# A product of the last matmul goes back from two levels of splitting to one, and the attention steps of the fourth unit are laid in another order

## The chip, the cores and the metric

One core of one Trainium2 chip runs the whole kernel. Times are device microseconds of that core. TensorE multiplies into PSUM[...], VectorE and ScalarE take the sums out of PSUM and do the elementwise work, and SyncE issues nearly all DMA transfers from one queue.

## The reference, cut to what matters

An attention without softmax is followed by a block of two matrix products with a squared relu between them. All arrays are fp32.

```python
kv  = einsum('bhsd,bhse->bhde', k, v)             # batch 8, heads 8, seq 576, head_dim 64
out = einsum('bhsd,bhde->bhse', q, kv)
out = out / sqrt(mean(out * out, -1) + 1e-6) * g_norm
x   = out.transpose(0, 2, 1, 3).reshape(4608, 512)
h   = x @ w_in                                    # 512 -> 2048
g   = s * maximum(h, 0) ** 2 + b
y   = g @ w_out                                   # 2048 -> 512
```

## The kernel before

The 4608 rows are cut into 36 chunks of 128, four chunks to a unit, so there are 9 units, numbered 0 to 8. The fourth unit is unit 3. In a unit the kernel does two big products, and inside the first it prepares the four attention chunks of the next unit.

Both products use a scheme of Winograd's: the matrices are cut into 2 x 2 blocks, sums of blocks are formed on VectorE, and seven block products take the place of eight. The first product (`mm1`) runs over four slices `s` of 512 columns. Its block products are named x1, z2, x6, y7, x5, x3 and y4 after the PSUM tiles x, y and z that they add into; block 3 of a slice and block 4 follow in the next slice, and for the last slice they follow in `rest()` below.

The second product (`mm2`) has seven block products too, numbered 1 to 7. From unit 2 on, six of them (1, 2, 6, 7, 4 and 3) are split a second time in the same way, into seven small products of 128 columns; only block 5 is done whole, with 256 columns for each of the two halves `j` of the rows. The second level of one block is made by `second_level`. `sums` forms the sums of the left matrix on VectorE, and `m1` to `m4` do the small products:

```python
def sums(which=(5, 6, 7, 3)):                 # each one is a 128x512 operation of VectorE
    ...
def go(m, bank, first):                       # four matmuls of 128 columns
    ...
    for f in range(FC // 4):
        matmul(t[bank], a[m][:, f], w[:, f], first and f == 0, f == FC // 4 - 1)

def keep(name, j, q):                         # a copy out of bank x, scaled, plus another term
    r[name] = late["tmp"].tile([P, P], FP32, name="r", tag="r")
    scaled(r[name], t["x"], other(j, cols[q]))

def m1(): go(1, "x", True);  keep("r1", 0, 0)
def m2(): go(2, "z", True);  scaled(to(0, cols[0]), t["z"], r["r1"])
def m6(): go(6, "x", False); keep("r2", 1, 0)          # adds to what m1 left in x
def m7(): go(7, "y", True)
def m5(): go(5, "x", False); keep("r4", 1, 1); scaled(to(1, cols[1]), t["y"], r["r4"])
def m3(): go(3, "x", False); scaled(to(0, cols[1]), t["x"], other(0, cols[1]))
def m4(): go(4, "y", False); scaled(to(1, cols[0]), t["y"], r["r2"])
```

Products 1, 6, 5 and 3 add into one bank, and each partial sum is copied out before the next product adds to it. `scaled` is one SCALAR_TENSOR_TENSOR operation of VectorE (line 714).

The order of a unit's second product stands in `rest()`. `p1`, `p2`, `p6`, `p7`, `p3`, `p4` are the second levels of the blocks; `at(n)` puts in a step of the next unit's attention, `at(5)` the four sums of the next unit's x; `pump(n)` asks for the next n tiles of weights, in a ring of 7. Its last part, from unit 2 on:

```python
            p7[2](); pump(1)
            p7[6]()
            p3["sums"]((5, 6))
            p7[7](); pump(1)
            p7[5]()
            at(3)
            p3["sums"]((7, 3))
            at("sums")
            p7[3](); pump(1)
            p7[4](); pump(1)
            with_5(0)                         # o1 += o2, the part from block 5
            at(("q", 0))
            p3[1](); p4["sums"]((5, 6)); at("norm")
            p3[2](); with_5(1); pump(1)
            p3[6](); p4["sums"]((7, 3))
            p3[7](); pump(1)
            p3[5]()
            at(4)
            p4[1]()
            p3[3](); store("o1", 0, 4 * u); pump(1)
            p3[4](); store("o1", 1, 4 * u + 1); pump(1)
            at(5)                             # the four sums of the next unit's x
            p4[2]()
            p4[6]()
            with_7(0)
            p4[7]()
            with_7(1)
            p4[5](); pump(2)
            at(("q", 1))
            y4_of(0, 3); pump(1)              # p4[3] and a store of o2
            y4_of(1, 4); pump(1)              # p4[4] and a store of o2
            at(("q", 2))
```

The attention steps of the next unit stand in a table: the key is (slice, place in the slice), and the places are 0 before x1, 1 after z2, 2 after x6 and 3 after y7. `turn` transposes q of a chunk on VectorE, `product` multiplies with kv on TensorE and squares on ScalarE, `row_sum` and `norm` (a square root on ScalarE, a reciprocal and a product on VectorE) divide, and `turn_x` transposes the result back on VectorE; for every second chunk four scalings with g_norm on ScalarE follow. In the last slice of a unit p1's four sums are laid after y7, ahead of place 3.

Of the kernel before, what the change touches and what calls it, by code (L numbers as in the profile page):

```python
# [16 lines left out]
def kernel(  # L17
# [39 lines left out]
    nc = tc.nc  # L57
# [231 lines left out]


    w2_dram = [dram.tile([P, FC // 2, HN], FP32, name=f"w2_{i}") for i in range(8)]
    TWICE = (1, 2, 6, 7, 4, 3)
    w3_dram = {
        i: dram.tile([P, 7, FC // 4, P], FP32, name=f"w3_{i}") for i in TWICE
    }
# [100 lines left out]
    def attention(c, first=False):  # L396
# [32 lines left out]
        def product(with_sum=True):  # L429
            if first:  # L430
                ps = bank_of("att", "xy"[c % 2]).rearrange("p b (m n) -> p (b m) n", m=2)
            else:
                pool, tag = (ps_f, "y") if c == 17 or c > 19 and c % 2 else (ps_a, "x")
                ps = pool.tile([P, NP, P], FP32, name="x_ps", tag=tag)
            if c < 2:
                for p in range(NP):
                    matmul(ps[:, p, :], st["qT"][:, p, :], bd_kv[0][:, p, :], True, True)
            for w in range(4 if c >= 2 else 0):
                for p in range(NP):
                    nc.tensor.matmul(  # L440
                        ps[32 * p : 32 * p + 32, w, :],
                        lhsT=st["qT"][:, p, 32 * w : 32 * w + 32],
                        rhs=bd_kv[(b if w < 2 else b1) % 2][:, p, :],
                        start=True,
                        stop=True,
                    )
            st["x"] = ps.rearrange("p c (l d) -> p (c l) d", l=2)
            st["xn"] = attp.tile([P, H, D], FP32, name="xn", tag="xn")
            nc.scalar.activation(st["xn"], st["x"], AF.Square)
            if with_sum:  # L450
                row_sum()
# [94 lines left out]
    def relu_sq(t):  # L546
        nc.vector.scalar_tensor_tensor(t, t, 0.0, t, ALU.max, ALU.mult)  # L547
# [38 lines left out]
    def mm1(u, s):  # L586

        st = {}

        def keep(name, src, tag):  # L590
            st[name] = rp.tile([P, 2, TB], FP32, name=name, tag=tag)
            nc.scalar.copy(st[name], src)  # L592

        def x1():
            st["x"] = bank_of("x", "x")
            mm1_product(1, u, s, st["x"], True)
            keep("r1", st["x"], "ra")

        def z2():
            ps = bank_of("z", "z", 1)  # L600
            mm1_product(2, u, s, ps, True)
            t = g_tile("a11", s)
            add(t, ps, st["r1"])
            relu_sq(t)

        def x6():
            mm1_product(6, u, s, st["x"], False)
            keep("r2", st["x"], "rb")

        def y7():  # L610
            st["y"] = bank_of("y", "y")
            mm1_product(7, u, s, st["y"], True)

        def x5():
            mm1_product(5, u, s, st["x"], False)
            keep("r4", st["x"], "ra")
            t = g_tile("a22", s)
            add(t, st["y"], st["r4"])
            if u > 1 and s == NS - 1:
                nc.scalar.activation(t, t, AF.Relu)  # L620
                nc.scalar.square(t, t)
            else:
                relu_sq(t)

        def x3():
            mm1_product(3, u, s, st["x"], False)
            nc.scalar.activation(g_tile("a21", s), st["x"], AF.Relu)

        def x3_square():
            if u > 1 and s == NS - 1:  # L630
                nc.scalar.square(ga["a21", s], ga["a21", s])
            else:
                nc.vector.tensor_mul(ga["a21", s], ga["a21", s], ga["a21", s])

        def x3_s1():
            g_tile("s1", s)
            g_s1(s)

        def x3_s3():
            sub(ga["a21", s], ga["a11", s], ga["a21", s])  # L640

        def y4():
            mm1_product(4, u, s, st["y"], False)
            add(g_tile("a12", s), st["y"], st["r2"])

        def y4_square():
            relu_sq(ga["a12", s])

        return dict(
            x1=x1, z2=z2, x6=x6, y7=y7, x5=x5, x3=x3, x3_square=x3_square, x3_s1=x3_s1,  # L650
            x3_s3=x3_s3, y4=y4, y4_square=y4_square,
        )
# [41 lines left out]
    def mm2(u, step=None, side={}):  # L694
# [9 lines left out]
        def product(i, j, ps, first):  # L704
            for f in range(FC // 2):
                s, b = divmod(f, 2)
                w2 = W2_AT[i][:, f] if u == 0 else ring[u, i, f // 4][:, f % 4]
                matmul(
                    ps, ga[G_OF[i], s][:, b, j * P : j * P + P], w2,
                    first and f == 0, f == FC // 2 - 1,  # L710
                )

        def scaled(o, ps, other):
            nc.vector.scalar_tensor_tensor(o, ps, s_col, other, ALU.mult, ALU.add)  # L714
# [165 lines left out]
            if last(j):  # L880
                store("o2", j, 4 * u + 2 + j, slice(HN, DM))

        def x3(j):
            product(3, j, st["x", j], False)
            scaled(rows("o1", j)[:, HN:], st["x", j], b2 if u == 1 else st["o1", j][:, HN:])
            store("o1", j, 4 * u + j)

# [42 lines left out]
        if u == 1:  # L930
            return [
                seq(lambda: x1(0), lambda: parts_of_w(1)),
                seq(lambda: x1(1), lambda: pump(2), s2),
                seq(lambda: z2(0), lambda: parts_of_w(2)),
                seq(lambda: z2(1), lambda: pump(2), s4),
                seq(lambda: x6(0), lambda: parts_of_w(6)),
                seq(lambda: x6(1), lambda: pump(2)),
                seq(lambda: y7(0), lambda: parts_of_w(7)),
                seq(lambda: y7(1), lambda: pump(2)),
                lambda: x5(0),  # L940
                seq(lambda: x5(1), lambda: pump(2)),
                seq(lambda: x3(0), lambda: parts_of_w(3)),
                seq(lambda: x3(1), lambda: pump(2)),
                seq(lambda: y4(0), lambda: parts_of_w(4)),
                seq(lambda: y4(1), lambda: pump(2)),
            ]

        def right(name, j, q=slice(0, HN)):
            return rows(name, j)[:, HN:][:, q]
# [8 lines left out]
            4, lambda j, q: st["r2"][:, j, q], lambda j, q: rows("o2", j)[:, q], "t", "t"  # L958
        )

        p3 = second_level(3, lambda j, q: right("o1", j, q), lambda j, q: right("o1", j, q), "x")

        def x5_of(j, *between):
            st["x", j] = half(("x", j), "x")
            product(5, j, st["x", j], True)
            for fn in between:
                fn()
            scaled(right("o2", j), st["x", j], b_21)

        def with_5(j):  # L970

            add(right("o1", j), right("o1", j), right("o2", j))

        def with_7(j):

# [11 lines left out]
        def rest():  # L987
# [7 lines left out]
            pump(1)  # L995
            p1[5]()
            step["x3"]()
            step["x3_square"]()
            p2["sums"]()
            p1[3]()  # L1000
            pump(1)
            p1[4]()
            pump(1)
            at(0)
# [33 lines left out]
            s4((3,))  # L1038
            p6[4]()
            pump(1)  # L1040
            p7["sums"]((3,))
            p7[2]()
            pump(1)
            p7[6]()
            p3["sums"]((5, 6))
            p7[7]()
            pump(1)
            p7[5]()
            at(3)
            p3["sums"]((7, 3))  # L1050
            at("sums")
            p7[3]()
            pump(1)
            p7[4]()
            pump(1)
            with_5(0)
            at(("q", 0))
            p3[1]()
            p4["sums"]((5, 6))
            at("norm")  # L1060
            p3[2]()
            with_5(1)
            pump(1)
            p3[6]()
            p4["sums"]((7, 3))
            p3[7]()
            pump(1)
            p3[5]()
            at(4)
            p4[1]()  # L1070
            p3[3]()
            store("o1", 0, 4 * u)
            pump(1)
            p3[4]()
            store("o1", 1, 4 * u + 1)
            pump(1)
            at(5)
            p4[2]()
            p4[6]()
            with_7(0)  # L1080
            p4[7]()
            with_7(1)
            p4[5]()
            pump(2)
            at(("q", 1))
            y4_of(0, 3)
            pump(1)
# [186 lines left out]
    def sides(u):  # L1274
# [34 lines left out]
        else:  # L1309
# [8 lines left out]
            if u > 3:  # L1318
                first[1, 2] = [*turn[2:], *row_sum[:2]]
                first[2, 0] = [*turn_x[:2], *q[1]]  # L1320
                first.update({
                    (2, 1): product[2:],
                    (2, 2): row_sum[2:],
                    (2, 3): norm[2:],
                    (3, 0): [turn_x[2]],
                    (3, 1): [turn_x[3]],
                })
            else:
                first[2, 0] = [*turn_x[:2], turn[2]]
                first.update({  # L1330
                    (2, 1): [product[2], row_sum[2]],
                    (2, 2): [norm[2]],
                    (2, 3): [turn_x[2], turn[3], *q[1]],
                    (3, 0): [product[3], row_sum[3]],
                    (3, 1): [norm[3]],
                    (3, 2): [turn_x[3]],
                })
        second[5] = [lambda: [sums() for sums in x_sums(u + 1)]]
        return first, second
# [92 lines left out]
```

## Time and profile before

| what | before |
|---|---|
| time, median of 3 | 971.71 us (970.51 to 973.76) |
| span of the profiled execution | 968.4 us |
| granted TensorE clock | 0.999 |
| VectorE SCALAR_TENSOR_TENSOR, 128x128 out of PSUM | 0.35 us |
| VectorE SCALAR_TENSOR_TENSOR, 128x256 out of PSUM | 0.48 us |
| VectorE sum, 128x512 | 0.69 us |
| ScalarE copy out of PSUM, 128x512 | 0.58 us |
| a 512 KB tile of weights, issue to landing | 4.6 us (median) |

In the timeline a fp32 matmul leaves two records, so a group of four matmuls is written as x8. Names in the profile are those of the program with the numbers left out: `sub` are the sums that `sums` makes, `w_sb` is a tile of weights in the ring (`w2_sb` in the program), `r` a kept partial sum, `a` one of the tiles a11 to a22 of the first product's result. Line 91 is the helper through which nearly all matmuls go, line 440 the attention's product, line 714 `scaled`, line 818 the stores of the output.

### The profile page before, as it was taken

What the parts mean: (1) busy time and instruction counts of PE and PEld (TensorE: products, weight loads), DVE (VectorE), ACT (ScalarE), POOL (GpSimd) and SP (SyncE); (2) the same over time, 40 slices, a digit from 0 to 9 for tenths busy, and PEclk for the clock granted to TensorE, in tenths of its full rate; (3) what the DMA queues carried; (4) which work ended last, traced back from release to release, by engine and by line L of the source; (5) the groups of instructions that cost most, each with busy time, mean ns of one, the idle gap of its engine ahead of it and who ended that gap; (6) DMA issues with size and microseconds to landing.
All of it is one profiled execution on the core that took longest, in us unless ns stands there. A gap on an engine that the chain in (4) does not pass through costs nothing.

```text
span 968.4 us, 18270 instructions
## 1 busy us (share of the span) xinstructions
PE 938.0 (97%) x7438; PEld 842.9 (87%) x7438; DVE 659.6 (68%) x1220; ACT 204.8 (21%) x387; POOL 6.7 (1%) x18
## 2 busy tenths in 40 slices
PE   7999999999999999999999999999999999999997
PEld 6888888888889988888889988998889888988996
DVE  2789766586658855777477856785678667864585
ACT  3773132112231013300231013201330032001100
POOL 2000000000000000000000000000000000000000
PEclk9999999999999999999999999999999999999999
DMA  9688736588863775167544754377427800681075
GB/s 238 209 303 247 247 88 180 132 282 229 233 178 110 244 193 154 18 219 226 143 102 146 253 172 112 111 245 210 110 53 243 249 20 12 219 263 52 19 220 165
DMA packets 140835, 165.85 MB, mean 171 GB/s; under 512 B 78032, under 2 KB 93648, under 8 KB 140624
## 3 DMA queue, kind: packets, MB, share of 16 engines
q1 hardware_dynamic: 137648, 162.91, 56.8%
q10 hardware_dynamic: 2784, 1.77, 0.8%
q8 instruction: 59, 0.97, 0.4%
q14 instruction: 24, 0.20, 0.1%
q0 software_dynamic: 320, 0.00, 0.0%
HBM read 136.84 MB, written 27.79 MB: 170 GB/s over the span
## 4 chain that ended last, share of the span: by engine, by line
PE 81%; DVE 10%; DMA 4%; ACT 2%; issue 1%; SPq 1%; DVEq 0%; ACTq 0%
PE x_ps L91 36%; PE y_ps L91 25%; PE z_ps L91 8%; PE t_ps L91 7%; PE x_ps L440 3%; DMA w_sb<-w 2%; DVE xs L250 2%; PE kv_ps L377 1%; DVE r L714 1%; DMA w_raw<-in_moe_w_in_dram 1%; DVE sub L250 1%; ACT xT L494 1%; DMA kv_sb<-in_k_dram 1%; DVE xT L488 1%; DVE a L247 1%
## 5 line engine op out<-in xcount | busy, mean ns | idle before, releaser
L592 ACT COPY r<-x_ps 128x512 f32<-128x512 f32 x96 | 56.0, 583 | 419.2 <-PE x_ps L91 396.9
L91 PE MATMUL x_ps<-xs,ws 128*128 128x256 f32 x512 | 122.1, 381 | 0.8 <-ACT r L592 0.4
L91 PE MATMUL y_ps<-xs,wb 128*128 128x256 f32 x512 | 122.6, 382 | 0.3 <-DVE a L247 0.3
L91 PEld LDWEIGHTS x_ps<-xs,ws 128*128 128x128 f32 x512 | 96.4, 190 | 15.9 <-ACT r L592 2.8
L91 PEld LDWEIGHTS y_ps<-xs,wb 128*128 128x128 f32 x512 | 95.5, 190 | 16.0 <-DVE a L247 2.5
L247 DVE TENSOR_TENSOR a<-y_ps,r 128x512 f32<-128x512 f32 x64 | 43.8, 685 | 76.7 <-ACT r L592 59.9
L91 PE MATMUL x_ps<-xT,wa 128*128 128x256 f32 x384 | 89.8, 380 | 0.1
L91 PEld LDWEIGHTS x_ps<-xT,wa 128*128 128x128 f32 x384 | 72.2, 190 | 10.5 <-ACT xT L494 0.5
L91 PE MATMUL y_ps<-w_sb,sub 128*128 128x128 f32 x560 | 70.1, 276 | 2.7 <-DVE r L714 2.7
L91 PEld LDWEIGHTS y_ps<-w_sb,sub 128*128 128x128 f32 x560 | 66.4, 192 | 4.4 <-DVE r L714 3.8
L91 PE MATMUL t_ps<-w_sb,sub 128*128 128x128 f32 x448 | 56.9, 278 | 8.0 <-DVE r L714 8.0
L547 DVE SCALAR_TENSOR_TENSOR a<-a 128x512 f32<-128x512 f32 x89 | 61.5, 691 | 2.8
L91 PEld LDWEIGHTS t_ps<-w_sb,sub 128*128 128x128 f32 x448 | 52.7, 192 | 10.5 <-DVE r L714 10.5
L91 PE MATMUL y_ps<-w_sb,a 128*128 128x128 f32 (+1 forms) x416 | 61.1, 295 | 0.0
L91 PE MATMUL x_ps<-xT,ws 128*128 128x256 f32 x256 | 60.5, 379 | 0.0
L91 PE MATMUL z_ps<-xT,wa 128*128 128x256 f32 x256 | 60.5, 379 | 0.0
L91 PE MATMUL x_ps<-w_sb,s 128*128 128x256 f32 x256 | 58.2, 380 | 1.9 <-DMA w_sb<-w 1.9
L91 PEld LDWEIGHTS y_ps<-w_sb,a 128*128 128x128 f32 x416 | 55.4, 192 | 2.2 <-issue 0.2
L91 PEld LDWEIGHTS x_ps<-w_sb,s 128*128 128x128 f32 x256 | 47.4, 190 | 8.4 <-issue 1.6
L91 PEld LDWEIGHTS z_ps<-xT,wa 128*128 128x128 f32 x256 | 48.7, 190 | 6.6
L91 PEld LDWEIGHTS x_ps<-xT,ws 128*128 128x128 f32 x256 | 48.1, 190 | 6.2
L250 DVE TENSOR_TENSOR a<-a,a 128x512 f32<-128x512 f32 x72 | 48.6, 685 | 0.8
(143 smaller groups left out, 1303.5 us busy)
## 6 DMA issues: line engine op xcount, KB each, us to landing
w_sb<-w SPq DMA_DIRECT2D x154, 512.0 KB, 4.6
w_sb<-w SPq DMA_DIRECT2D x42, 256.0 KB, 3.4
w_raw<-in_moe_w_in_dram SPq DMA_DIRECT2D x8, 1024.0 KB, 8.7
w_raw<-in_moe_w_out_dram SPq DMA_DIRECT2D x8, 1024.0 KB, 5.2
w_sb<-in_k_dram SPq DMA_DIRECT2D x48, 144.0 KB, 3.0
w_sb<-in_v_dram SPq DMA_DIRECT2D x48, 144.0 KB, 3.0
out_dram<-o SPq DMA_DIRECT2D x104, 64.0 KB, 2.7
w<-sub SPq DMA_DIRECT2D x24, 256.0 KB, 3.7
```

The costliest lines, as they stand in the source:

```text
L91: nc.tensor.matmul(o, lhsT=lhsT, rhs=rhs, start=start, stop=stop, skip_group_check=True)
L247: nc.vector.tensor_tensor(out=o, in0=a, in1=b, op=ALU.add)
L250: nc.vector.tensor_tensor(out=o, in0=a, in1=b, op=ALU.subtract)
L377: nc.tensor.matmul(ps[r][l * HB : l * HB + HB, i, :], lhsT=kv[l][rows, 0, j, :], rhs=kv[l][rows, 1, j, :], start=(j == 0), stop=(j == R - 1),)
L440: nc.tensor.matmul(ps[32 * p : 32 * p + 32, w, :], lhsT=st["qT"][:, p, 32 * w : 32 * w + 32], rhs=bd_kv[(b if w < 2 else b1) % 2][:, p, :] ...
L488: nc.vector.transpose(out=to, in_=st["xn"].rearrange("p h d -> p (h d)").rearrange("p (c x) -> p c x", c=KC))
L494: nc.scalar.activation(to[:, i], to[:, i], AF.Copy, scale=g_col[:, i : i + 1])
L547: nc.vector.scalar_tensor_tensor(t, t, 0.0, t, ALU.max, ALU.mult)
L592: nc.scalar.copy(st[name], src)
L714: nc.vector.scalar_tensor_tensor(o, ps, s_col, other, ALU.mult, ALU.add)
```

## The change

Two things are exchanged. Block 3 of the second product is no longer split a second time: two plain products of eight matmuls with 256 columns (one for each j) take the place of seven small ones with 128 columns, and they add to what block 5 left in their two x banks. The first is laid between p7[5] and p7[3], the second between p4[5] and p4[3]. And in unit 3 the attention steps for the next unit are laid out in another order. The split of block 3 in two levels was made to save multiplications; its absence saves sums on VectorE and weight traffic, and gives pieces of work of TensorE that depend on no copy. The new order in unit 3 is meant to have q of its last chunk turned before TensorE asks for it.

```diff
-    TWICE = (1, 2, 6, 7, 4, 3)
+    TWICE = (1, 2, 6, 7, 4)
...
-                pool, tag = (ps_f, "y") if c == 17 or c > 19 and c % 2 else (ps_a, "x")
+                pool, tag = (ps_f, "y") if c > 16 and c % 2 else (ps_a, "x")
...        (x5: relu and square of a22)
-            if u > 1 and s == NS - 1:
-                nc.scalar.activation(t, t, AF.Relu)
-                nc.scalar.square(t, t)
-            else:
-                relu_sq(t)
+            relu_sq(t)                       # one operation of VectorE
...        (x3_square)
-            if u > 1 and s == NS - 1:
-                nc.scalar.square(ga["a21", s], ga["a21", s])
-            else:
-                nc.vector.tensor_mul(ga["a21", s], ga["a21", s], ga["a21", s])
+            nc.vector.tensor_mul(ga["a21", s], ga["a21", s], ga["a21", s])
...
-        def x3(j):
+        def x3(j, *between):
             product(3, j, st["x", j], False)
+            for fn in between:
+                fn()
+            if u > 1:
+                add(right("o1", j), right("o1", j), b_21)
             scaled(rows("o1", j)[:, HN:], st["x", j], b2 if u == 1 else st["o1", j][:, HN:])
             store("o1", j, 4 * u + j)
...        (unit 1: the sums of block 3's weights and their seven transfers)
-                seq(lambda: x3(0), lambda: parts_of_w(3)),
+                lambda: x3(0),
...        (rest(): x3_square() moves from before p2["sums"]() to after p1[3]())
...        (rest(), from p7[2] on; the lines with p3 and with_5 shown above go)
             p7[2]()
             p7[6]()
             p7[7]()
             p7[5]()
             at(3)
+            def between():
+                p7["sums"]((3,))
+                p4["sums"]()
+                at("sums")
+                p7[3]()
+                pump(1)
+                p7[4]()
+                pump(1)
+                at(("q", 0))
+                p4[1]()
+                at("norm")
+
+            x3(0, between)
             p4[2]()
             p4[6]()
             with_7(0)
             p4[7]()
             with_7(1)
             p4[5]()
-            pump(2)
+            at(4)
+            at(5)
+            x3(1)
+            pump(4)
             at(("q", 1))
             y4_of(0, 3)
...        (attention of unit 3)
-                    (2, 1): [product[2], row_sum[2]],
-                    (2, 2): [norm[2]],
-                    (2, 3): [turn_x[2], turn[3], *q[1]],
-                    (3, 0): [product[3], row_sum[3]],
-                    (3, 1): [norm[3]],
-                    (3, 2): [turn_x[3]],
+                    (2, 1): [turn[3], product[2]],
+                    (2, 2): [row_sum[2], *q[1]],
+                    (2, 3): [norm[2]],
+                    (3, 0): [product[3], turn_x[2]],
+                    (3, 1): [row_sum[3]],
+                    (3, 2): [norm[3]],
+                    (3, 3): [turn_x[3]],
```

`q[1]` in the table is the issue of q's loads for unit 5. Their first chunk goes into the buffer that chunk 19's q leaves free when it has been turned.

More of the change, by code (lines that the diff above doesn't have):

```diff
@@ L959, in mm2 @@
         )
-        p3 = second_level(3, lambda j, q: right("o1", j, q), lambda j, q: right("o1", j, q), "x")
         def x5_of(j, *between):
@@ L968, in x5_of @@
             scaled(right("o2", j), st["x", j], b_21)
-        def with_5(j):
-            add(right("o1", j), right("o1", j), right("o2", j))
         def with_7(j):
@@ L997, in rest @@
             step["x3"]()
-            step["x3_square"]()
             p2["sums"]()
@@ L1001, in rest @@
             pump(1)
+            step["x3_square"]()
             p1[4]()
@@ L1040, in rest @@
             pump(1)
-            p7["sums"]((3,))
             p7[2]()
@@ L1044, in rest @@
             p7[6]()
-            p3["sums"]((5, 6))
             p7[7]()
@@ L1049, in rest @@
             at(3)
[L1050 to L1077, printed above, removed]
+            def between():
[10 more added lines that the diff above has]
+            x3(0, between)
             p4[2]()
```

## The prediction

> **What bounds the kernel now.** I read the page's busy shares first, then the waits of TensorE, then TensorE in order of time, and last VectorE and the DMA queue where TensorE stands still.
>
> ```profile
> PE 938.0 (97%) x7438; PEld 842.9 (87%) x7438; DVE 659.6 (68%) x1220; ACT 204.8 (21%) x387; POOL 6.7 (1%) x18
> ```
>
> TensorE is the bound. Time is won or lost in two ways only: fewer columns through it, or fewer gaps in it. Its waits in total (us, times, longest):
>
> ```profile
> PE t_ps L91 <- DVE r L714: 8.0, 13, 0.9
> PE y_ps L91 <- DVE r L714: 2.7, 6, 0.4
> PE x_ps L440 <- DVE qT L409: 2.0, 3, 0.9
> PE x_ps L91 <- DMA w_sb<-w: 1.9, 2, 1.3
> ```
>
> The first two rows sit in the second-level products at the end of units 2 to 8. TensorE in unit 3 in order of time (start, length, group; x8 is one group of four fp32 matmuls, each recorded twice):
>
> ```profile
> 389.15 1.99 PE L91 MATMUL x_ps<-xs,ws 128*128 128x256 f32 x8 [0.38 <-ACT r L592]
> 391.75 1.08 PE L440 MATMUL x_ps<-bd_kv,qT 128*32 128x128 f32 x32 [0.60 <-DVE qT L409]
> ...
> 420.55 1.97 PE L91 MATMUL x_ps<-w_sb,s 128*128 128x256 f32 x8 [1.26 <-DMA w_sb<-w]
> 423.14 1.99 PE L91 MATMUL x_ps<-w_sb,s 128*128 128x256 f32 x8 [0.64 <-DMA w_sb<-w]
> ...
> 438.25 2.84 PE L91 MATMUL y_ps<-w_sb,sub 128*128 128x128 f32 x24
> 441.54 1.16 PE L91 MATMUL y_ps<-w_sb,sub 128*128 128x128 f32 x8 [0.45 <-DVE r L714]
> ...
> 447.30 1.16 PE L91 MATMUL x_ps<-w_sb,sub 128*128 128x128 f32 x8
> ...
> 451.87 1.95 PE L91 MATMUL t_ps<-w_sb,sub 128*128 128x128 f32 x16
> 454.63 1.16 PE L91 MATMUL t_ps<-w_sb,sub 128*128 128x128 f32 x8 [0.81 <-DVE r L714]
> 456.24 1.16 PE L91 MATMUL t_ps<-w_sb,sub 128*128 128x128 f32 x8 [0.45 <-DVE r L714]
> 457.23 1.06 PE L91 MATMUL t_ps<-w_sb,a 128*128 128x128 f32 x8
> 458.12 1.89 PE L91 MATMUL x_ps<-xT,wa 128*128 128x256 f32 x8
> ```
>
> Undisturbed groups give the pitch: those of 128 columns start at 448.30, 449.19, 450.08, 450.98 and 451.87, so 0.893 us each; seven of 256 columns fill 351.49 to 363.58, so 1.727 us each. From p7's sixth product (438.25) to the next unit (458.12) lie 19.87 us. They hold 5 groups of p7, 7 of p3 and 7 of p4: 19 x 0.893 = 16.98 us. So 2.89 us are gaps, more than the 1.71 us listed, as the short ones and part of each listed one hide in the recorded length. The four gaps are product 3 after product 5 in p7 and in p3 (before 447.30), and products 5 and 3 of p4. Units 4 to 7 repeat it to within 0.02 us a line.
>
> VectorE shows the cause of the longest:
>
> ```profile
> 451.45 0.68 DVE L250 TENSOR_TENSOR xs<-xT 128x512 f32<-128x512 f32 x1
> ...
> 453.37 0.69 DVE L250 TENSOR_TENSOR xs<-xT,xs 128x512 f32<-128x512 f32 x1
> 453.98 0.34 DVE L714 SCALAR_TENSOR_TENSOR o<-z_ps,s_col,r 128x128 f32<-128x128 f32 x1
> 454.24 0.34 DVE L714 SCALAR_TENSOR_TENSOR r<-t_ps,s_col,or 128x128 f32<-128x128 f32 x1
> ```
>
> The four sums of x for the next unit stand ahead of the copy that p4's fifth product needs. The tail of the launch is the output queue, not TensorE:
>
> ```profile
> 956.00 9.93 SPq L818 DMA_DIRECT2D out_dram<-o  x18
> ```
>
> Eighteen stores at 0.55 us each run without a break to 965.9, 3.4 us after TensorE's end at 962.5.
>
> [...]groups last 1.06 us at a pitch of 0.893. Hence I count from start to start. [...]products 6, 5 and 3 add into one bank and each must wait for a copy out of it. [...]256 columns take 1.727 us, 3% less than twice 0.893.
>
> **The change, part by part.**
>
> 1. *Product 3 loses its second level in units 2 to 8.* Removed: 7 groups of 128 columns, 6.25 us. Added: two plain products of two 256-column groups, 4 x 1.727 = 6.91 us. TensorE pays 0.66 us a unit.
>
> 2. *The plain product's halves fall into the gaps.* The new order is p7[5], 3.45 us of product 3 for j=0, p7[3], p7[4], p4[1], [2], [6], [7], [5], 3.45 us for j=1, p4[3], p4[4]. So 3.45 us now stand behind each product 5, which must wait for nothing, while VectorE makes its copy (0.35 us). The x sums move behind p4[5], and their 2.5 us lie under the second half. p3's own gap is gone with it. In the first half VectorE owes two evacuations and five sums, about 3.6 us, of which only one sum is needed at once. At p4[5] the copy after p4[6] has 0.89 us and now has nothing queued ahead of it. New length: 12 x 0.893 + 6.91 = 17.63 us for 19.87: 2.24 us won in each of units 3 to 7, 11.2 in all. Unit 2 takes 21.27 us (330.22 to 351.49) less about 1.0 for an attention product, so 2.6; I take 0.2 off for the division that stands before p4's copies: 2.4. Unit 8 has no x sums; from 943.59 to 962.38 are 18.79 us, so 1.81 of gap less 0.66: 1.15. Together 14.75 us.
>
> 3. *Unit 3's attention.* q of chunk 19 is turned two places sooner, so the wait at 391.75 goes, and with the square root a place later the one at 389.15. From 386.88 to 392.76 are 5.88 us for two 1.73 products and about 1.0 of attention: 1.4 won. The q loads for unit 5 wait for that turn (the queue shows 4.6 us of waiting for qT, then loads to 415.6), and the weights at 420.55 come behind them. Turned some 8 us sooner, the queue is free about 4.6 us sooner: from 416.44 to 424.98 are 8.54 us for 6.13 of work, so 2.4 won.
>
> 4. *A new stall in unit 3.* Chunk 19 is now turned back behind p1's four sums on VectorE, and its four scalings (1.7 us) stand on ScalarE ahead of the r4 copy. I move the old times up by about 1 us: row sum 399.55, a12 400.15 to 400.8, division and product to 402.6, sums to 405.2, turn to 405.8, scalings to 407.65, r4 to 408.2, a22 to 408.95. y4 adds into the bank that a22 reads and would be due at 406.2: 2.8 us lost. Chunk 19 also takes a y bank, so y7 needs the bank that a12 releases at 400.83, due at 400.5: 0.4. With the start of two fresh groups (0.15 each) 3.5 us.
>
> 5. *Off the path.* Relu and two squares of the last slice go from ScalarE to VectorE, two operations of 0.69 us; VectorE stands idle 1.4 us before a12 (408.66) and in 0.54 us pieces later, so TensorE sees nothing. Unit 1 loses four sums and seven transfers of 256 KB, where TensorE shows no such wait. The ring brings 24 tiles a unit for 26.
>
> 6. *The tail.* Product 3 for j=1 ends 1.8 us before TensorE, so its four stores now stand ahead of the last six: from about 1.1 us before TensorE's end ten stores take 5.5 us, to 4.4 after it, for 3.4 before. 1.0 lost.
>
> Sum: -14.75 - 1.4 - 2.4 + 3.5 + 1.0 = -14.05 us. I keep 1.4 back for gaps that I haven't seen: -12.7, or 959.0 us from 971.7.
>
> **The rivals.** (a) *Only the arithmetic counts*: seven times 0.66 is paid and the gaps reappear at other products. For it: VectorE was busy at every gap. Against: p6, whose fifth and third product are already held apart by p7[1], shows no gap between them in any unit. It makes 971.7 + 4.6 + 3.5 + 1.0 less 3.8 from unit 3, so 977. (b) *The weights become the wait*: product 3's second tile is asked for when p6[3] ends and used 6.2 us later, where tiles land in 4.6 us at the median and took up to 10 behind unit 3's q loads. For it: the two waits at 420.55. Against: 5.4 us is the longest landing in unit 4's window around it. It costs about 1 us a unit: 966. (c) *Unit 3's stall is absent*: VectorE or ScalarE gets there sooner than I reckon; 3.5 us less, 955.5. (d) *Part 3 alone works*, the second level having been well hidden before; the four gaps per unit speak against it.
>
> **Range and chances.** The range 954 to 966 holds (c) with a little more, and (b) in full; (a) lies outside, and I give it 5%. Faster by over 2% needs 952.3, beyond all gaps counted: 4%. Slower by over 2% needs 991.1, for which nothing in the profile speaks: 1%. Within 2%: 95%.
>
> **What would show it.** After the change the waits of t_ps and y_ps on r should fall from 10.7 us to under 1, the time from p7[6] to the next unit from 19.87 to 17.6, the waits on w_sb to 0, and y_ps should wait near 3 us once, for a22 in unit 3. TensorE's busy time should grow by about 4 us less what its overlapping records hide. Wrong would be: gaps of 0.4 us or more that come back behind p4[6] or p7[5], waits of x_ps for w_sb in every unit, or a span in which units 4 to 7 stay 2 us above the length reckoned here.

## The result and the profile after

The changed kernel takes 956.3 us (median of 6 runs, 955.7 to 957.7) for 971.5 before: a ratio of 0.984, with a 95% interval of 0.983 to 0.985. Predicted were 959.0, in a range of 954 to 966. The span of the profiled execution falls from 968.4 to 955.1 us.

The page's busy shares after, and the longest of TensorE's waits (us, times, longest one):

```profile
PE 936.7 (98%) x7270; PEld 840.1 (88%) x7270; DVE 639.9 (67%) x1167; ACT 191.6 (20%) x366; POOL 6.7 (1%) x18
```

```profile
PE y_ps L91 <- DVE a L247: 2.9, 3, 2.4
...
PE x_ps L440 <- DVE qT L409: 0.5, 1, 0.5
...
PE x_ps L91 <- ACT r L592: 0.4, 1, 0.4
```

In the second product no bank (a PSUM tile of 128 partitions x 512 fp32 columns) waits for a kept partial sum any more (10.7 us before in the rows of t_ps and y_ps, 1.0 in that of x_ps), nor for w_sb; the last row shown is a wait of the first product. At the top stands one new wait of 2.4 us. TensorE in unit 3 after, in order of time:

```profile
386.77 1.99 PE L91 MATMUL x_ps<-xs,ws 128*128 128x256 f32 x8 [0.39 <-ACT r L592]
388.69 1.08 PE L440 MATMUL x_ps<-bd_kv,qT 128*32 128x128 f32 x32
...
398.81 1.99 PE L91 MATMUL y_ps<-xs,wb 128*128 128x256 f32 x8 [0.21 <-DVE a L247]
...
406.73 2.86 PE L91 MATMUL y_ps<-xs,wb 128*128 128x256 f32 x8 [2.41 <-DVE a L247]
409.38 1.89 PE L91 MATMUL x_ps<-w_sb,sub 128*128 128x128 f32 x8
...
420.87 3.62 PE L91 MATMUL x_ps<-w_sb,s 128*128 128x256 f32 x16
...
437.61 2.84 PE L91 MATMUL y_ps<-w_sb,sub 128*128 128x128 f32 x24
440.29 3.62 PE L91 MATMUL x_ps<-w_sb,a 128*128 128x256 f32 x16
443.74 1.05 PE L91 MATMUL y_ps<-w_sb,sub 128*128 128x128 f32 x8
...
449.99 3.62 PE L91 MATMUL x_ps<-w_sb,a 128*128 128x256 f32 x16
453.45 1.05 PE L91 MATMUL t_ps<-w_sb,sub 128*128 128x128 f32 x8
...
455.23 1.89 PE L91 MATMUL x_ps<-xT,wa 128*128 128x256 f32 x8
```

From p7's sixth product (437.61) to the next unit (455.23) are 17.62 us for 19.87 before. The halves of product 3 (440.29 and 449.99) stand where the gaps were, and no line there has a wait. The weights at 420.87 are there in time. New is the pause before 406.73, and the groups behind it are slower than elsewhere in the unit: four matmuls of 256 columns take 2.65 us from start to start for 1.73, four of 128 take 1.71 for 0.89.

Start to start of the units' first product, both traces:

| unit | before, us | after, us | difference | predicted |
|---|---|---|---|---|
| 2 | 104.91 | 101.69 | -3.22 | -2.4 |
| 3 | 106.63 | 106.07 | -0.56 | -2.5 |
| 4, 5, 6 | 103.18, 103.13, 103.14 | 100.91, 100.90, 100.89 | -2.27, -2.23, -2.25 | -2.24 each |
| 7 | 100.22 | 97.97 | -2.25 | -2.24 |
| 8 to the end | 100.61 | 99.17 | -1.44 | -0.15 |

The sum is -14.2 us. Unit 1 is the same, and the start of the launch was 0.9 us longer in this execution; in the thirteen traces of this study unit 1 begins between 140.7 and 143.4 us.

### The profile page after: what moved, and what is told of

Same layout as the page of the kernel before. It is cut to its first block, busy times and chain, and to the rows that moved or that the text cites. A ratio compares the mean times of both kernels' runs of the same rounds, so it can differ in the third digit from the quotient of the medians.

```text
span 955.1 us, 17793 instructions
## 1 busy us (share of the span) xinstructions
PE 936.7 (98%) x7270; PEld 840.1 (88%) x7270; DVE 639.9 (67%) x1167; ACT 191.6 (20%) x366; POOL 6.7 (1%) x18
## 4 chain that ended last, share of the span: by engine, by line
PE 88%; DVE 6%; ACT 3%; DMA 2%; issue 1%; SPq 0%; DVEq 0%; ACTq 0%
PE x_ps L91 41%; PE y_ps L91 26%; PE z_ps L91 8%; PE t_ps L91 8%; PE x_ps L440 3%; PE kv_ps L377 2%; DMA w_raw<-in_moe_w_in_dram 1%; ACT xT L494 1%; DMA kv_sb<-in_k_dram 1%; DVE a L247 1%; DVE a L250 1%; DVE xT L488 1%; DVE a L547 1%; DVE xn L463 1%; DVE sub L250 1%
## 5 line engine op out<-in xcount | busy, mean ns | idle before, releaser
L91 PE MATMUL x_ps<-w_sb,a 128*128 128x256 f32 (+1 forms) x376 | 79.7, 364 | 0.0
L91 PEld LDWEIGHTS x_ps<-w_sb,a 128*128 128x128 f32 x376 | 66.9, 190 | 8.4 <-issue 0.6
L547 DVE SCALAR_TENSOR_TENSOR a<-a 128x512 f32<-128x512 f32 x96 | 66.4, 691 | 3.1
L91 PE MATMUL y_ps<-w_sb,sub 128*128 128x128 f32 x504 | 62.0, 275 | 0.0
L91 PEld LDWEIGHTS y_ps<-w_sb,sub 128*128 128x128 f32 x504 | 60.3, 192 | 0.7
L91 PE MATMUL t_ps<-w_sb,sub 128*128 128x128 f32 x448 | 54.8, 275 | 0.0
L626 DVE TENSOR_TENSOR a<-a 128x512 f32<-128x512 f32 x32 | 22.0, 689 | 47.6 <-ACT a L623 47.6
L91 PE MATMUL y_ps<-w_sb,a 128*128 128x128 f32 (+1 forms) x360 | 53.7, 298 | 0.0
```

Source lines behind the costliest of these rows:

```text
L91: nc.tensor.matmul(o, lhsT=lhsT, rhs=rhs, start=start, stop=stop, skip_group_check=True)
```

## The experiments

Each ratio is to the kernel before, run beside it, with its 95% interval.

**1. Unit 3's attention alone.** Before, with the new order and its y bank:

```diff
-                    (2, 3): [turn_x[2], turn[3], *q[1]],
+                    (2, 1): [turn[3], product[2]],
...                  (all of the table and the tag of the y bank, as in the change)
+                    (3, 3): [turn_x[3]],
```

> The kernel before with only unit 3's attention in the new order (chunk 19 in a y bank too); product 3 keeps its second level. Theory A (the product's place is nearly all of the gain, unit 3's order is a wash): about 1 us won at the turn of q, 2.4 us won at the weights in unit 3, 4.4 us lost to the new stall before y4 and the slow clock after it, so 971 to 973 us, and the gaps behind p7[5] and p4[5] stay. Theory B (the attention's order carries the gain): 960 us or less.

Measured: 1.0024 (1.0013 to 1.0035). In the trace unit 3 takes 108.23 us for 106.63, the gaps of the small products stay in every unit, and the pause of 2.41 us before y4 is there. Theory B falls: alone, the new order costs some 2 us.

**2. Product 3 alone.** After, with unit 3's attention in the old order:

```diff
-                    (2, 1): [turn[3], product[2]],
+                    (2, 3): [turn_x[2], turn[3], *q[1]],
...                  (all of the table and the tag, back)
```

> The kernel after with unit 3's attention in the old order. Theory A: the gaps at t_ps and y_ps stay closed in all seven units, the stall before y4 in unit 3 goes (4.4 us won), the wait for qT (0.7 us) and the one for weights in unit 3 (about 2 us) come back: 954 to 957 us. Theory B: near 968 us.

Measured: 0.984 (0.982 to 0.986), 954.7 us, the same ratio as the whole change. No bank of the second product waits for r; the wait for qT (0.60) and two for weights (1.02 and 0.78) are back in unit 3, and y4 follows p1[2] with no pause. The change's time is that of this part, with the small moves that come with it (relu and squares on VectorE, no weights of block 3 in unit 1).

**3. The turn of chunk 19 moved out of the way.**

```diff
                     (3, 2): [norm[3]],
-                    (3, 3): [turn_x[3]],
                 })
+                second[3] = [turn_x[3]]      # behind p7[5]
```

> The kernel after with one step moved: the turn of chunk 19 with its four scalings goes from the last place of unit 3's last slice to behind p7[5]. If the pause before y4 also causes the 0.50 clock that follows it, both go: 2.6 us of wait and 1.7 us of slow matmuls, so 4.3 us less than the kernel after, 952 us. If the slow clock has another cause and stays, 2.6 us less: 953.7 us. If the pause was not ScalarE's scalings, no change.

Measured: 0.982 (0.980 to 0.984), 952.1 us. In the trace unit 3 takes 101.75 us for the 106.07 of the kernel after, 4.3 us less; pause and slow matmuls are both gone. In the timed runs it is 2 us less, with intervals as wide as that; experiment 10 and the last section show why the two may differ.

**4. Both halves of product 3 together.** The same work, another place:

```diff
+            p7["sums"]((3,)); p4["sums"](); at("sums")
+            p7[3](); p7[4](); at(("q", 0))
+            x3(0); x3(1); pump(2)
+            p4[1](); at("norm"); p4[2](); p4[6]()
...
             p4[5](); at(4); at(5)
-            x3(1)
-            pump(4)
+            pump(2)
```

> The kernel after with both halves of product 3 done together behind p7[4], so that p7[3] stands directly behind p7[5] and p4[3] directly behind p4[5]; x sums stay behind p4[5]. The same work on every engine. If the gain is the halves' place: the gaps of 0.61 and 0.72 us come back, 1.33 us in each of seven units, 9.3 us more: 965.5 us. If the gain is VectorE's lighter load (about 2.9 us less a unit): the gaps stay closed and it takes 956 us.

Measured: 0.9995 (0.9986 to 1.0004). All of the gain is gone, more than the 9.3 us expected. TensorE in unit 4 of this kernel, in order of time:

```profile
541.67 2.84 PE L91 MATMUL y_ps<-w_sb,sub 128*128 128x128 f32 x24
545.94 1.16 PE L91 MATMUL y_ps<-w_sb,sub 128*128 128x128 f32 x8 [1.43 <-DVE sub L250]
...
559.81 1.16 PE L91 MATMUL t_ps<-w_sb,sub 128*128 128x128 f32 x8 [0.44 <-DVE r L707]
```

The second gap is the expected one. The first is longer than before's, since p7[3] needs the last sum of p7, which the changed kernel forms behind p7[5]; there product 3's half covers it, here nothing does. VectorE at that place, the copy and then the sum:

```profile
544.55 0.35 DVE L707 SCALAR_TENSOR_TENSOR r<-y_ps,s_col,o 128x128 f32<-128x128 f32 x1 [1.44 <-PE y_ps L91]
...
545.21 0.68 DVE L250 TENSOR_TENSOR sub<-a,sub 128x512 f32<-128x512 f32 x1
```

p7[3] was due at 541.67 + 3 x 0.893 = 544.35. The copy alone, done at 544.90, would have held it up by 0.55 us, and the sum adds the rest. VectorE is busy 638.7 us, as in the kernel after (639.9). So it is the place and not the lighter load of VectorE that closes the gaps, and the half covers a sum besides a copy.

**5. Before, with x sums behind p4[5].**

```diff
-            at(5)
             p4[2]()
             p4[6]()
...
             p4[5]()
+            at(5)
```

> The kernel before with one step moved: the four sums of the next unit's x go from ahead of p4[2] to behind p4[5]. If they hold up the copy that p4's fifth product waits for, the gap of 0.97 us goes in units 2 to 7, 5.8 us won: 0.994 of the kernel before, and the gaps of product 3 behind product 5 stay. If the copy is late for another reason, no change.

Measured: 0.9931 (0.9916 to 0.9946), 6.7 us won for 5.8 expected. TensorE's waits for r in this kernel:

```profile
PE t_ps L91 <- DVE r L714: 3.1, 7, 0.4
PE y_ps L91 <- DVE r L714: 2.7, 6, 0.4
```

The t_ps row falls from 13 waits and 8.0 us to 7 and 3.1; what is left are the third products directly behind the fifth. So nearly half of the gain is to be had in the kernel before by moving one line.

**6. Two levels kept, the small products interleaved.** Before, with the last part reordered:

```diff
             p7[5]()
+            p4[1]()
             p7[3](); p7[4]()
+            p4[2]()
             p3[1](); p3[2](); p3[6](); p3[7](); p3[5]()
+            p4[6]()
             p3[3]()
             p4[7](); p4[5]()
+            p3[4]()
+            at(5)
```

> The kernel before, product 3 still in two levels (0.66 us a unit less work for TensorE than the kernel after), with the small products of p7, p3 and p4 laid between each other so that none stands directly behind the copy it needs, and x sums behind p4[5]. If the place alone makes the gain: 2.9 us won in each of units 2 to 7 and 1.8 in unit 8, some 19 us, less the stores at the end: 0.980 to 0.982, better than the kernel after but for unit 3. If VectorE's load makes gaps anywhere (it has some 16 us of work for 17 us of TensorE there), 0.985 to 0.992.

Measured: 1.028 (1.026 to 1.030). One wait explains it, with what follows it:

```profile
PE t_ps L91 <- DMA w_sb<-w: 24.7, 7, 4.1
```

p4[1] asked for its tile of weights seven products sooner than before, and the ring had not brought it yet. Behind six of the seven waits matmuls run at half speed: groups of 128 columns start up to 1.87 us apart for 0.893, and the first four groups behind each of the six cost another 12.8 us in all. The mean granted clock of the execution is 0.983, for 0.999 before. The order of products had been changed, and not that of their transfers: a mistake of this experiment, and no verdict on the idea.

**7. The same with the turn moved as in 3.**

> The interleaved kernel with unit 3's new order and chunk 19's turn behind p7[5], as in the run with the turn moved. If the gains add: 3.2 us less than the interleaved kernel (the waits for qT and for weights in unit 3), 0.977 to 0.979. If VectorE is too full behind p7[5], as much as without it or more.

Measured: 1.025 (1.024 to 1.027), 994.6 us for the 997.8 of experiment 6. That is the 3.2 us expected, but with 26.8 us of the same wait, 12.4 us lost to slow groups behind it and a mean granted clock of 0.984 it says no more than 6 about the interleaving.

**8. Two of the four scalings later.**

```diff
+                now = 2 if c == 19 else KC
+                for i in range(now):
+                    scale(i)
+                late["scalings"] = [partial(scale, i) for i in range(now, KC)]
...
+                second[0] = [lambda: [fn() for fn in late["scalings"]]]
```

> The kernel after with two of chunk 19's four scalings moved behind the copy of x5 on ScalarE. The pause before y4 in unit 3 gets 0.85 us shorter, 1.75 us recorded for 2.6. If the clock of 0.50 after it comes only from pauses longer than that, it goes too: 0.85 + 1.7 = 2.6 us less than the kernel after. If any pause of this kind brings it, 0.85 us less and the slow matmuls stay.

Measured: 0.984 (0.982 to 0.985). In the trace the pause is 1.62 us for 2.41, the clock stays at 1.00, and unit 3 takes 103.77 us, 2.3 less than in the kernel after. The length of the pause follows the scalings, as reckoned. That the slow clock went with it fits the last section: past the first 25 us, the pauses listed there with slow matmuls behind them lasted 2.41 us or more. The timed ratio doesn't resolve the 2.3 us.

**9. Interleaved, with the weights in the order of use.**

```diff
-        for i in ORDER if u == 1 else (1, 2, 5, 6, 7, 3, 4):
+        for i in ORDER if u == 1 else (1, 2, 5, 6, 7):
...
+            for i, n in ((4, 0), (3, 0), (3, 1), (3, 2), (4, 1), (4, 2), (3, 3), (4, 3))
```

> The interleaved kernel once more, two levels for product 3, with p4's first tile of weights asked for ahead of p3's (in the runs before it came 4 us late in every unit), p4's sums moved back behind p3's, and unit 3's attention as in the run with the turn moved. If the late tile was all that cost, TensorE has 19 small groups without gaps at the end of a unit, 16.98 us for the 17.63 of the kernel after: 4.6 us less than with the turn moved, 0.977 of the kernel before. If VectorE or the ring is too full for it, gaps come back and it is no better than 0.982.

Measured: 0.9805 (0.978 to 0.983), the lowest ratio of all. No wait for weights is left, and none for r in the second product is listed; one short gap is, between the second and third of these lines:

```profile
440.49 1.06 PE L91 MATMUL y_ps<-w_sb,sub 128*128 128x128 f32 x8
441.38 1.06 PE L91 MATMUL x_ps<-w_sb,sub 128*128 128x128 f32 x8
442.42 1.16 PE L91 MATMUL t_ps<-w_sb,sub 128*128 128x128 f32 x8
```

Units 5 and 6 take 100.51 and 100.49 us for 100.90 and 100.89: 0.4 won a unit of the 0.66 that a second level saves. Unit 8 with the stores took 1.7 us more than in experiment 3. Against 3 the two intervals overlap, so this is the fastest version by its ratio, and not shown to be faster than 3.

**10. The weights of block 3 prepared for nothing.**

```diff
-                lambda: x3(0),
+                seq(lambda: x3(0), lambda: parts_of_w(3)),   # nothing reads them
```

> The kernel after with the four sums of block 3's weights and their seven transfers to memory put back into unit 1; nothing reads them. If they held up q's loads, the wait of TensorE for q's turn in unit 2 (0.9 us before, none after) comes back and the time grows by about 1 us. If that wait went for another reason, no change.

Measured: 0.984 (0.982 to 0.986). The time doesn't resolve 1 us. The trace does; TensorE in this kernel:

```profile
277.18 1.08 PE L440 MATMUL x_ps<-bd_kv,qT 128*32 128x128 f32 x32 [1.34 <-DVE qT L409]
...
406.55 1.99 PE L91 MATMUL y_ps<-xs,wb 128*128 128x256 f32 x8 [2.41 <-DVE a L247]
408.38 1.05 PE L91 MATMUL x_ps<-w_sb,sub 128*128 128x128 f32 x8
```

The first line is the wait that the change had removed: unit 2 takes 103.11 us here for 101.69. VectorE shows what the turn of q waited for:

```profile
276.32 0.71 DVE L409 STREAM_TRANSPOSE qT<-q_sb 128x512 f32<-128x512 f32 x1 [3.53 <-DMA q_sb<-in_q_dram]
```

In the kernel before it waited 3.14 us for its loads, in the kernel after not at all. So that work in unit 1 held up q's loads. The other two lines were not expected: the same pause of 2.41 us as in the kernel after, and this time full speed behind it. Unit 3 takes 104.41 us.

**11. The kernel after once more.**

> The kernel after itself, beside the other two on one chip: 0.984 of the kernel before, with the pause before y4 in unit 3 and the 0.50 clock behind it as in its first trace. If the slow clock was chance, it is gone here.

Measured: 0.984 (0.982 to 0.986), with the pause of 2.41 us and a clock of 0.50 behind it, unit 3 106.23 us.

## Why the prediction was right, point by point

*Product 3's work and the gaps (parts 1 and 2).* Right to 0.03 us a unit in units 4 to 7: 2.24 predicted, 2.23 to 2.27 measured. Experiments 2 and 4 show that it is this part and the place of the halves, and 5 that x sums held up the fifth product. In unit 2 the end came to 2.21 us (330.10 to 349.16 for 330.22 to 351.49) where 2.4 stood; the 0.2 us that I took off for the division is there, in a group of products that lasts 3.08 us for 2.84.

*Unit 3's attention (part 3).* The weights: 2.4 us predicted; 6.14 us from 418.19 to 424.33 for 8.54, so 2.4 won. The turn: of 1.4 us only 0.7 came (384.49 to 389.70, 5.21 us for 5.88). The wait at 389.15 stayed, at 386.77 now, and the step that failed is its cause. I gave it to the square root ahead of it on ScalarE. The copy r2 itself was late, in both kernels behind VectorE's a, before first, then after:

```profile
388.51 0.58 ACT L592 COPY r<-x_ps 128x512 f32<-128x512 f32 x1 [4.30 <-DVE a L247]
```

```profile
386.13 0.59 ACT L592 COPY r<-x_ps 128x512 f32<-128x512 f32 x1 [4.30 <-DVE a L247]
```

`r2` has one buffer, and the a12 of the slice before must have read it. The square root now comes after that copy, and nothing changed. On VectorE a step of the attention stands directly ahead of that a12 in both: the row sum before (387.15), the turn of chunk 19 after (384.76).

*The new stall (part 4).* Right in kind and nearly in size: 3.5 us for both places, 0.3 of it an estimate for the start of the two groups behind the pauses. In experiment 10, where the clock stays up, y7 starts 0.4 and y4 2.6 us late, and the first group behind each pause lasts 0.1 us longer (1.99 for 1.89): 3.1 or 3.2. VectorE and ScalarE after come in the order reckoned, about 2.2 us earlier on the clock than reckoned, as does the time when y4 is due (404.15 for 406.2):

```profile
403.04 0.71 DVE L488 STREAM_TRANSPOSE xT<-xn 128x512 f32<-128x512 f32 x1
405.98 0.69 DVE L247 TENSOR_TENSOR a<-y_ps,r 128x512 f32<-128x512 f32 x1 [2.24 <-ACT r L592]
```

```profile
403.78 1.70 ACT L494 ACTIVATE xT<-xT,g_col 128x256 f32<-128x256 f32 x4 [4.14 <-DVE xT L488]
405.39 0.56 ACT L592 COPY r<-x_ps 128x512 f32<-128x512 f32 x1
```

Four scalings stand ahead of the copy, and the sum behind it. That the copy would come behind the scalings was my estimate from the trace of before, where four sums on VectorE stand ahead of the copy at 454.24; here it starts at 405.39, within 0.1 us of the end of the scalings (403.78 and 1.70). So rival (c) falls. What I hadn't was the clock behind the pause. With it unit 3 takes 106.07 us, without it 104.41 (experiment 10), and 104.37 with the old order (experiment 2): without the slow clock the new order in unit 3 wins and loses the same.

*Off the path (part 5).* VectorE's added relu and square left no wait. Wrong was that unit 1's lighter load is worth nothing: the wait of 0.94 us for qT in unit 2 went, as experiment 10 shows. I had looked for such waits in unit 1, and that work delayed loads for the unit behind it.

*The tail (part 6).* Mis-sized: 1.0 us predicted, none lost. The line of 18 stores includes the queue's waits; the single stores, before and after, in nanoseconds:

```profile
L818 SPq DMA_DIRECT2D out_dram<-o x18: 315/420/1401, 956.0 to 965.5; - x18
```

```profile
L811 SPq DMA_DIRECT2D out_dram<-o x18: 315/421/435, 941.9 to 952.4; - x18
```

A store takes 0.42 us to issue, not 0.55. The last ten after run from 948.26 to 952.79, 3.3 us past TensorE's end at 949.5, where it was 3.4 before.

*The rivals.* (a) falls, since the gaps came back nowhere; (b) falls, since nothing waits for w_sb; (d) is refuted by experiment 1. *The sum*: what I kept back for unseen gaps, 1.4 us, wasn't needed, and the errors of unit 2 (0.8 us too little), the tail (1.0 too much lost), the turn (0.7 too much won) and the clock (1.7 not foreseen) nearly cancel. That the traces' total of 14.2 us comes so close to the 14.05 reckoned is luck. One of the signs was badly chosen: TensorE's busy time did not grow by 4 us but fell by 1.3. A recorded group ends some 0.17 us after its pitch (1.06 for 0.893), and each gap lays that much of it bare; the group behind a gap is recorded 0.1 us longer too (1.16 for 1.06). Four gaps make 1.1 us a unit, more than the 0.66 that the added columns cost: TensorE is busy in unit 4 for 101.18 us before and 100.79 after. Where gaps close, this busy time is no measure of work.

## What to carry to other kernels

Where products add into one bank and a copy must come between them, look for independent work of the bound engine to lay there: two pieces of 3.45 us of plain products, with the x sums moved, won 2.24 us a unit, though the pieces cost 0.66 more than what they replaced. About 1.1 us a unit is to be had by moving the sums alone (experiment 5). Read such gaps from start to start. When products are reordered, reorder their transfers with them, and look at what stands ahead of the copy on the copying engine: four sums in the wrong place cost 1 us a unit, four scalings 2.7 us.

## What the runs showed of the hardware

The slow matmuls behind the pause are the clock. The windows of the kernel after (us, busy time of each engine with its instructions, PEclk, DMA share, GB/s):

```profile
406.00:407.00 1.00, 0.27 (x1) 0.28 (x2) 0.97 (x2) 0.00 (x0) 0.00 (x0) 1.00 0.24 37
407.00:408.00 1.00, 1.00 (x5) 0.90 (x5) 0.90 (x3) 0.00 (x0) 0.00 (x0) 0.85 0.23 35
408.00:409.00 1.00, 1.00 (x4) 0.73 (x4) 0.11 (x1) 0.00 (x0) 0.00 (x0) 0.50 0.22 34
...
410.00:411.00 1.00, 1.00 (x7) 1.00 (x6) 0.32 (x1) 0.00 (x0) 0.00 (x0) 0.50 0.15 22
411.00:412.00 1.00, 1.00 (x11) 1.00 (x10) 0.69 (x2) 0.00 (x0) 0.00 (x0) 0.94 0.53 53
```

The granted clock falls to 0.50 here about 1 us after TensorE has started again at 406.73, and stays there for some 3.4 us (0.3 of a us in the second window, three whole ones, 0.1 in the last). That made unit 3 1.7 us longer. In experiment 1 the slow stretch also lasts 3.4 us, but the fall comes 0.2 us before TensorE starts again at 408.88 (a mean clock of 0.83 from 408 to 409 and of 0.96 from 412 to 413, 0.50 between); in experiment 11 it lasts 3.4 us too (0.70 from 408 to 409, 0.59 from 411 to 412, 0.50 between).

The waits of 2.41 to 2.48 us in seven traces were followed by matmuls at half speed in four (the kernel after twice, experiments 1 and 4) and not in three (experiment 10, and unit 2 of 6 and 7). The twelve waits of 3.52 us and more in experiments 6 and 7 were all followed by them. Those of 1.43 us (4), 1.62 us (8) and 1.80 us (6) were not. In the first 25 us, where TensorE waits several times in a row, the length does not tell: 1.24 us (8), 1.47 us (11) and 1.64 us (6) were followed by slow matmuls (a group of four records in 1.06 us for 0.60), 2.21 us (the kernel after) was not.

The windows of experiment 10, with a pause as long as in the kernel after:

```profile
404.00:406.00 2.00, 0.14 (x2) 0.00 (x0) 0.19 (x1) 1.77 (x5) 0.00 (x0) 1.00 0.22 33
406.00:407.00 1.00, 0.45 (x2) 0.42 (x3) 0.97 (x2) 0.00 (x0) 0.00 (x0) 1.00 0.25 37
407.00:408.00 1.00, 1.00 (x7) 0.87 (x6) 0.84 (x3) 0.00 (x0) 0.00 (x0) 1.00 0.24 35
408.00:409.00 1.00, 1.00 (x9) 0.95 (x8) 0.42 (x1) 0.00 (x0) 0.00 (x0) 1.00 0.27 44
409.00:410.00 1.00, 1.00 (x11) 1.00 (x11) 0.80 (x3) 0.00 (x0) 0.00 (x0) 1.00 0.16 23
```

Why a pause of 2.41 us brings the slow clock in one execution and not in another, no run here shows. Of the five traces with this pause before y4, four had it. Moving the turn (experiment 3) is then worth 2.7 us in some executions and 4.3 in the others; the 2 of its timed runs, with their intervals, do not speak against that.
